# Three edits to a fused attention and two-MLP kernel: scale of w1 from a sum of squares, the product with the values in float16 halves, and a new table of ranks

## The chip, the cores and the metric

The kernel runs on one core of a Trainium2 chip. The metric is the device time of one execution in microseconds (us); lower is better. Before the change the median of three runs is 1182.09 us (1180.85 to 1185.35).

## The reference

Inputs q, k, v have the shape (8 batches, 8 heads, 576 rows, 64). All is float32.

```python
# chunked attention: 9 chunks of 64 rows, each attends to itself only
scores = (q_c @ k_c.T) / 8
attn = exp(scores - max); attn = attn / (sum(attn) + 1e-9)
x = attn @ v_c                              # to (8, 576, 512), heads side by side
# first MLP
xn = (x - mean) / sqrt(var + 1e-6) * g1
x = x + relu(xn @ w1) @ w2                  # w1: 512 x 2048, w2: 2048 x 512
# second MLP with a gate along the rows
h = gelu_tanh(x @ w_in); u, v = halves of h
v = norm(v) * g2;  v = w_sg @ v + b_sg      # w_sg: 576 x 576
out = x + (u * v) @ w_out
```

## The kernel before, in words

The 4608 rows of x are 36 tiles of 128 rows (`t`), two to a block of 256 rows (`b`, 18 blocks). A float32 matrix that enters a large product is split into two float16 halves, high and low, and a product is three float16 products: high by high, high by low, low by high. From block 4 on the first MLP, and in the second MLP the product with w_in, run as seven products of half the size (the lists `POS` and `SIDES`). One function builds the program. Nothing is issued in the order of the source: `op(engine, ns, fn, rd, wr, prio)` (L59) records each step with its engine, an assumed duration, what it reads and writes, and a rank. `Plan.run` (L88) then plays the steps through by the assumed durations and, at each time when an engine is free, issues the ready step with the lowest rank. The ranks of the first eight tiles and of the weight pieces stand in the table `TUNE` (L24 to 42). Every engine runs its own list in order, so a step that waits holds all later steps of its engine.

**Attention** (`attention`, L300 to 437). For a tile, q and k arrive by a DMA, 16 products of 64 by 64 give the scores in PSUM (`qk`, L291), VectorE takes row maxima and subtracts them (L371, L372), ScalarE takes the exponential (L375). The result must be turned for the product with v. Up to tile 13, TensorE does it (`pt_`, L334) and ScalarE copies it from PSUM (L396). From tile 14 on (22 tiles) ScalarE rounds it to float16 (the high half of `ph`), VectorE makes the low half (L383), a DMA transposes both (`ptt`, L386), and VectorE adds the halves to a float32 tile again (`pt`, L389). The product with v (`pv_`, L343) is 16 float32 products of 64 by 64, each of which TensorE runs as two passes, each with a weight load of its own. They use the four 64 by 64 quadrants of the array: partitions 0 to 63 or 64 to 127 of the operands by partitions 0 to 63 or 64 to 127 of the output. The row sums are taken by VectorE (L393), or for tiles 0 to 3 by a product with a column of ones (`sums`, L366); a reciprocal (L360) and a product (L410) give x. `norm` (L439) computes mean and variance (L442, L443), the inverse root on POOL (GpSimd, L437, L440), the normalized tile on VectorE or POOL (L446), its two float16 halves (L449, L451), and a DMA transposes them to `xT` (L266). From tile 10 on the product with v of one tile and the scores of the next are one step.

**w1** (`make_w1`, L481). Eight pieces of 256 columns. A piece arrives as raw 64-bit words and is converted by ScalarE and VectorE (L466, L471). For its scale, ScalarE (L489, seven pieces) or VectorE sums or bounds the magnitudes on each partition. `par` (L243) makes one number of the 128: a product with the unit matrix that turns the column to a row (`turn`, L223), a maximum on VectorE (`rowmax`, L227), a product that spreads it to 128 partitions (`spread`, L231), a copy (`floor`, L239). VectorE cuts it to a power of two, takes its reciprocal and scales g1 with it (L257, L258, L501). Then the piece is multiplied by that column and split into `w1h` and `w1l` (L510, L514 in the direct form). `scale_w2` (L556) later uses the pieces' scales for w2.

**The first product** (`ff1`, L596) takes 12 products of 128 by 128 by 256 for each group of 128 columns; two groups use one piece. Where the planner sees TensorE idle in the start, `busy` (L1162) puts products of zeros (L1165), one for each 150 ns of the expected idle time beyond 400 ns, until the third PSUM bank is used the first time (`plan.idle = None`). From there on none is added.

Of the kernel before, what the change touches and what calls it, by code (L numbers as in the profile page):

```python
# [9 lines left out]
F16 = mybir.dt.float16  # L10
# [14 lines left out]
    a=[2264, -1991, -1698, -26, -1734, 4025, 2562, -374],  # L25
    w=[2426, 2508, 9, 2951, 1823, 2431, -436, 2455],
    w2=[2013, 747, 2422, -1063, 2355, -444, 700, 2423],
    an=[-135, -91, -57, -1323, -88, -1232, 366, 0],
    wb=[0, -1141, 0, -402, 109, -61, 1242, 1022],
    lo=[1, 0, 0, 0, 0, 1, 1, 1],  # L30
    wl=[1, 1, 1, 1, 1, 1, 1, 0],
    wc=[0, 1, 0, 1, 1, 1, 0, 1],
    wa=[1, 1, 1, 1, 0, 1, 1, 1],
    wm=[0, 0, 1, 0, 0, 0, 0, 1],
    ps=[1, 1, 1, 1],
    wf=[1, 1, 1, 1, 1, 0, 0, 1],
# [110 lines left out]
def fused_kernel(ctx: ExitStack, tc, qkv, w1, w2, g1, w_in, w_out, wsgt, wsgs, g2, b_sg, out):  # L147
    nc = tc.nc
    PSUM = bass.MemoryType.PSUM
    P = 128  # L150
# [46 lines left out]
    g1m = small.tile([P, 2], F32, name="g1m")  # L197
    redw = small.tile([P, 8], F32, name="redw")
    invw = small.tile([P, 8], F32, name="invw")
    gsw = small.tile([P, 8, 4], F32, name="gsw")  # L200
    e1c = small.tile([P, 8], F32, name="e1c")
# [99 lines left out]
    def attention(t):  # L301
# [22 lines left out]
        pt = palloc("pt", 1, [P, 4, 128], F32)  # L324
# [5 lines left out]
        pv = s2[:, :, 256:512].rearrange("p a (h d) -> p a h d", h=4)  # L330

# [6 lines left out]
        def pv_():  # L338
            for hp in range(4):
# [38 lines left out]
        else:  # L378
            ph = palloc("ph", 1, [P, 2, 512], F16)
            ptt = palloc("ptt", 1, [P, 2, 512], F16)  # L380
# [38 lines left out]
    def norm(t, x, o):  # L419
# [16 lines left out]
        def rs_():  # L436
# [7 lines left out]
        o("POOL", 730, rs_, rd=[mv, "cpow"], wr=[rs], two=2)  # L444
        xe = ("POOL", 830, nc.gpsimd) if t < 8 and TUNE['xn'][t] else ("DVE", 460, nc.vector)
        o(xe[0], xe[1], lambda: xe[2].tensor_scalar(  # L446
            out=xn.t, in0=x.t, scalar1=mv.t[:, 0:1], scalar2=rs.t, op0=ALU.subtract, op1=ALU.mult
        ), rd=[x, mv, rs], wr=[xn], two=1 + (xe[0] == "POOL"))
# [32 lines left out]
    def make_w1(j):  # L481
# [4 lines left out]
        e, inv, gs = e1c[:, j:j + 1], invw[:, j:j + 1], gsw[:, j]  # L486
        wv = lambda: w.t.rearrange("p (k f) -> p k f", k=4)
        if TUNE['wa'][j]:
            op("ACT", 1056, lambda: nc.scalar.activation(  # L489
                out=w1h[j].bitcast(BF16), in_=wv(), func=AF.Abs, scale=g1m[:, 1:2], accum_out=redw[:, j:j + 1]  # L490
            ), rd=[w, "g1m"], wr=[f"mxw{j}", f"w1h{j}"], prio=pr)
        else:
            op("DVE", 1127, lambda: absmax(redw[:, j:j + 1], w.t), rd=[w], wr=[f"mxw{j}"], prio=pr)
            op("DVE", 78, lambda: nc.vector.tensor_tensor(
                out=redw[:, j:j + 1], in0=redw[:, j:j + 1], in1=g1m[:, 0:1], op=ALU.mult
            ), rd=["g1m"], wr=[f"mxw{j}"], prio=pr)
# [1154 lines left out]
```

## Time and profile before

| | us |
|---|---|
| median of three runs | 1182.09 |
| lowest and highest run | 1180.85, 1185.35 |
| the profiled execution: its own time | 1181.42 |
| its span in the profile | 1179.6 |
| TensorE products (PE), busy in the span | 1168.0 |
| VectorE (DVE) | 866.1 |
| ScalarE (ACT) | 564.2 |
| GpSimd (POOL) | 268.3 |

Busy time is the time in which an instruction of the engine runs. Products on PE are pipelined: their starts are recorded, their ends are modelled, so a row's duration is longer than its distance to the next start. The distance of starts is what a product costs where PE never stops. PE stands for products, PEld for weight loads, which run beside them.

### The profile page before, as it was taken

How to read it: one execution, taken by the hardware profiler on the slowest of the kernel's cores; microseconds unless marked ns; L12 is line 12 of the kernel's file. 1: busy time of each engine (PE TensorE's matmuls, PEld its weight loads, DVE VectorE, ACT ScalarE, POOL GpSimd, SP SyncE). 2: the span in 40 equal slices, each digit the busy share in tenths (PEclk: the TensorE clock that was granted, in tenths of full speed). 3: DMA queues.
4: the chain of work that ended last, by engine and by line, in shares of the span. 5: the costliest groups of instructions: out<-in, count | busy, mean ns of one | idle time of the engine just before them, and what ended most of it. 6: DMA issues, size and time to landing. Idle time of an engine off the chain costs nothing.

```text
span 1179.6 us, 26988 instructions
## 1 busy us (share of the span) xinstructions
PE 1168.0 (99%) x11387; PEld 879.9 (75%) x11387; DVE 866.1 (73%) x1673; ACT 564.2 (48%) x830; POOL 268.3 (23%) x318
## 2 busy tenths in 40 slices
PE   8899999999999999999999999999999999999998
PEld 6688654688888888888888888888565556556454
DVE  6996114999898898888877775677899479477455
ACT  5787501555655665644344334445646335434330
POOL 2213401434312322331221312013303102202300
PEclk6999999999999999999999999999999999999999
DMA  7974002135572433343234221435284473262203
GB/s 278 282 239 126 1 18 81 64 108 156 164 161 67 82 86 76 88 95 93 84 81 91 55 55 28 87 89 167 57 176 128 102 147 112 87 124 73 89 1 116
DMA packets 165049, 124.30 MB, mean 105 GB/s; under 512 B 128704, under 2 KB 137792, under 8 KB 164928
## 3 DMA queue, kind: packets, MB, share of 16 engines
q1 hardware_dynamic: 164928, 122.58, 39.6%
q8 instruction: 89, 1.46, 0.5%
q14 instruction: 32, 0.26, 0.1%
HBM read 72.74 MB, written 18.88 MB: 78 GB/s over the span
## 4 chain that ended last, share of the span: by engine, by line
PE 96%; DVE 2%; DMA 1%; issue 0%; ACT 0%; SPq 0%; POOL 0%; DVEq 0%; ACTq 0%
PE bank L722 25%; PE acc L774 22%; PE bank L615 6%; PE pb L1446 5%; PE acc L1530 4%; PE pair L636 4%; PE bank L636 4%; PE pb L1530 4%; PE acc L1446 3%; PE pb L1350 3%; PE acc L1392 3%; PE pb L1392 3%; PE acc L1350 3%; PE pair L343 2%; PE pair L291 2%; PE pb L1447 1%
## 5 line engine op out<-in xcount | busy, mean ns | idle before, releaser
L722 PE MATMUL bank<-xT,w1h 128*128 128x256 f16 x1792 | 299.7, 273 | 0.0
L774 PEld LDWEIGHTS <-arena 128*128 128x128 f16 x2352 | 228.3, 98 | 27.6
L722 PE MATMUL bank<-xT,w1l 128*128 128x256 f16 x896 | 244.2, 273 | 0.0
L774 PE MATMUL acc<-w,arena 128*128 128x256 f16 x1344 | 202.7, 273 | 0.0
L722 PEld LDWEIGHTS <-w1h 128*128 128x128 f16 x1792 | 175.0, 98 | 20.5
L749 ACT ACTIVATE arena<-arena 128x896 f16<-128x896 f32 x112 | 106.3, 949 | 144.2 <-PE acc L774 84.8
L774 PE MATMUL acc<-w2s,arena 128*128 128x256 f16 x1008 | 165.4, 273 | 0.0
L750 DVE TENSOR_TENSOR arena<-arena 128x896 f16<-128x896 f32 x112 | 122.3, 1092 | 30.2 <-ACT arena L749 29.7
L737 ACT ACTIVATE arena<-bank 128x512 f32<-128x512 f32 x112 | 66.6, 594 | 129.7 <-PE bank L722 122.8
L722 PEld LDWEIGHTS <-w1l 128*128 128x128 f16 x896 | 87.7, 98 | 10.2
L615 PE MATMUL bank<-xT,w1h 128*128 128x256 f16 x512 | 86.2, 273 | 1.3 <-DMA xT<-hl 1.1
L807 POOL TENSOR_TENSOR x<-x,u 128x256 f32<-128x256 f32 (+1 forms) x60 | 53.5, 921 | 124.9 <-DVE x L797 89.4
L744 DVE TENSOR_TENSOR arena<-arena 128x256 f32<-128x256 f32 x112 | 54.7, 489 | 32.2 <-ACT arena L737 31.9
L437 POOL TENSOR_SCALAR rs<-mv 128x1 f32<-128x1 f32 x36 | 11.3, 313 | 284.0 <-DVE mv L443 267.3
L1350 PEld LDWEIGHTS <-x2T 128*128 128x128 f16 x672 | 65.6, 98 | 9.1 <-issue 0.2
L451 POOL TENSOR_TENSOR hl<-xn,hl 128x512 f16<-128x512 f32 x32 | 49.8, 1555 | 89.0 <-ACT hl L449 85.7
L615 PE MATMUL bank<-xT,w1l 128*128 128x256 f16 x256 | 69.8, 273 | 0.0
L615 PEld LDWEIGHTS <-w1h 128*128 128x128 f16 x512 | 48.6, 98 | 12.2 <-issue 1.6
L1446 PEld LDWEIGHTS <-vh 128*128 128x128 f16 x288 | 28.5, 99 | 33.4
L1530 PEld LDWEIGHTS <-gh 128*128 128x128 f16 x296 | 28.9, 98 | 31.6
L1297 POOL TENSOR_SCALAR rs<-mv 128x2 f32<-128x2 f32 (+1 forms) x20 | 5.8, 291 | 204.3 <-DVE mv L1292 204.1
L1446 PE MATMUL pb<-wsg,vh 128*128 128x512 f16 x166 | 51.6, 380 | 0.0
(300 smaller groups left out, 2293.0 us busy)
## 6 DMA issues: line engine op xcount, KB each, us to landing
straw<-in_w SPq DMA_DIRECT2D x16, 1023.8 KB, 5.7
qkl<-in_qkv SPq DMA_DIRECT2D x26, 512.0 KB, 4.0
x2d<-x SPq DMA_DIRECT2D x36, 256.0 KB, 2.1
xr<-x2d SPq DMA_DIRECT2D x35, 256.0 KB, 2.9
out<-xr SPq DMA_DIRECT2D x35, 256.0 KB, 3.1
xs<-x2d SPq DMA_DIRECT2D x27, 256.0 KB, 3.6
vl<-in_qkv SPq DMA_DIRECT2D x26, 256.0 KB, 3.2
qk<-in_qkv SPq DMA_DIRECT2D x10, 512.0 KB, 5.5
```

Source lines behind the costliest of these rows:

```text
L615: nc.tensor.matmul(acc, lhsT=w[j][:, k, fc], rhs=xT.t[:, x, k], start=(n == 0), stop=(n == 11))
L636: nc.tensor.matmul(acc[i], lhsT=h[x].t[:, c], rhs=w2t[j][:, f % 2, y], start=(f == 0 and n == 0), stop=(f == NF - 1 and n == 2),)
L722: nc.tensor.matmul(acc[:, y * 256:y * 256 + 256], lhsT=w[j][:, k, fc], rhs=xT.t[:, x, k], start=(n == 0), stop=(n == 11),)
L737: op("ACT", 500, lambda: nc.scalar.activation(out=o.t[:, 0:4].rearrange("p n t -> p (n t)"), in_=acc, func=AF.Relu, scale=0.5), rd=[kb] + ...
L744: nc.vector.tensor_tensor(out=two(6, 8), in0=two(1, 3), in1=two(0, 2), op=ALU.subtract)
L749: op("ACT", 860, lambda: nc.scalar.activation(out=h.t[:, 0], in_=o.t[:, 1:8], func=AF.Copy), rd=[o] + ar, wr=[h], prio=-100)
L750: op("DVE", 1010, lambda: nc.vector.tensor_tensor(out=h.t[:, 1], in0=o.t[:, 1:8], in1=h.t[:, 0], op=ALU.subtract), rd=[o, h], wr=[h.key + ...
L774: nc.tensor.matmul(acc, lhsT=h.t[:, x, n], rhs=r(y), start=(first and j == 0 and m == 0), stop=(j == 7 and m == 2), skip_group_check=True,)
L1350: nc.tensor.matmul(ap[:, q * 256:q * 256 + 256], lhsT=xT[:, x, a, k, c], rhs=right(b, 1, k, w), start=(first and n == 0), stop=(k == 1 and ...
L1392: nc.tensor.matmul(ap, lhsT=right(b, 0, k, w)[:, m * 128:m * 128 + 128], rhs=xT[:, x, a, k], start=(first and n == 0), stop=(k == 1 and w ...
L1446: nc.tensor.matmul(ap, lhsT=v[:, fc], rhs=w[:, 0:512], start=(n == 0), stop=end)
L1530: nc.tensor.matmul(ap[:, 0:m], lhsT=x[:, k, c], rhs=w[:, k, fc], start=(n == 0), stop=(n == 11))
```

## The change

Four edits, and new numbers in `TUNE`:

1. The scale of a w1 piece is taken from the sum of squares. ScalarE squares all eight pieces; one product with a 128 by 128 matrix of ones (`total`) adds the 128 partitions and leaves the sum on all of them; VectorE bounds it from below, POOL raises it to the power -0.5, VectorE scales g1. `turn`, `rowmax`, `spread` and the cut to a power of two go for w1; they stay for w2's one scale.
2. Of four of the first eight tiles the reciprocal of the row sums moves to POOL (`rp`, where the row sums come from VectorE), and for three the normalized tile is made on ScalarE (`xa`).
3. From tile 14 on the two transposed float16 halves are not added. v is split into float16 halves (`vq`: one copy on ScalarE, one subtraction on VectorE), and the product with v is three float16 products for each float32 one: 48 weight loads and 48 products in a tile where 16 float32 products of two passes stood.
4. Two of the first four tiles take their row sums by TensorE instead of four (`ps`).

```diff
 TUNE = dict(
-    a=[2264, -1991, -1698, -26, -1734, 4025, 2562, -374],
-    w=[2426, 2508, 9, 2951, 1823, 2431, -436, 2455],
+    a=[2627, 508, -2387, -855, 341, 2595, 604, 4055],
+    w=[3820, 3377, 142, 4188, 5125, 3910, 106, 2633],
...
-    ps=[1, 1, 1, 1],
-    wf=[1, 1, 1, 1, 1, 0, 0, 1],
+    xa=[0, 1, 0, 0, 0, 1, 0, 1],
+    rp=[0, 1, 1, 1, 0, 1, 1, 1],
+    ps=[0, 1, 0, 1],
+    wf=[1, 1, 1, 1, 0, 0, 0, 1],
...
         def pv_():
+            if t >= BYDMA:
+                for hp in range(4):
+                    for n, (y, z) in enumerate(((0, 0), (0, 1), (1, 0))):
+                        for r in (slice(0, 64), slice(64, 128)):
+                            for c in range(2):
+                                k = c * 256 + hp * 64
+                                q = hp * 128 + c * 64
+                                nc.tensor.matmul(
+                                    s2[64 * c:64 * c + 64, r.start // 64, 256 + hp * 64:256 + hp * 64 + 64],
+                                    lhsT=ptt[0].t[r, y, q:q + 64],
+                                    rhs=vq[0].t[r, z, k:k + 64],
+                                    start=(n == 0),
+                                    stop=(n == 2),
+                                )
+                return
...
-            ), rd=[ph], wr=[ptt], lat=3500)
+            ), rd=[ph], wr=[ptt[0]], lat=3500)
+            vq[0] = palloc("vq", 1, [P, 2, 512], F16)
+            o("ACT", 520, lambda: nc.scalar.activation(out=vq[0].t[:, 0], in_=v.t, func=AF.Copy), rd=[v], wr=[vq[0]])
             o("DVE", 600, lambda: nc.vector.tensor_tensor(
-                out=pt.t.rearrange("p h q -> p (h q)"), in0=ptt.t[:, 0], in1=ptt.t[:, 1], op=ALU.add
-            ), rd=[ptt], wr=[pt], two=1, **far)
+                out=vq[0].t[:, 1], in0=v.t, in1=vq[0].t[:, 0], op=ALU.subtract
+            ), rd=[v], wr=[vq[0]], two=1, **far)
...
+                def rp_():
+                    f = lambda x: x.t.rearrange("p h a o -> p (h a o)")
+                    nc.gpsimd.tensor_scalar(out=f(sm), in0=f(sm), scalar1=1.0, scalar2=1e-9, op0=ALU.mult, op1=ALU.add)
+                    nc.gpsimd.tensor_tensor(out=f(rd), in0=f(sm), in1=cneg.to_broadcast([P, 8]), op=ALU.pow)
...
-        if TUNE['wa'][j]:
-            op("ACT", 1056, lambda: nc.scalar.activation(
-                out=w1h[j].bitcast(BF16), in_=wv(), func=AF.Abs, scale=g1m[:, 1:2], accum_out=redw[:, j:j + 1]
-            ), rd=[w, "g1m"], wr=[f"mxw{j}", f"w1h{j}"], prio=pr)
...
-        par(e, redw[:, j:j + 1], [f"mxw{j}"], [f"e{j}"], pr)
-
-        def scale():
-            top2(e, inv)
-            nc.vector.tensor_scalar(out=gs, in0=g1s, scalar1=inv, scalar2=32.0, op0=ALU.mult, op1=ALU.mult)
-
-        op("DVE", 520, scale, wr=[f"e{j}"], prio=pr, two=1)
+        op("ACT", 1056, lambda: nc.scalar.activation(
+            out=w1h[j].bitcast(BF16), in_=wv(), func=AF.Square, scale=g1m, accum_out=redw[:, j:j + 1]
+        ), rd=[w, "g1m"], wr=[f"mxw{j}", f"w1h{j}"], prio=pr)
...
+        op("PE", 200, lambda: total(scr, redw[:, j:j + 1]), rd=[f"mxw{j}", "ident"], wr=[k], prio=top, lat=300)
+        op("DVE", 80, lambda: nc.vector.tensor_scalar_max(q, scr[:, P:P + 1], 2.0 ** -120), rd=[k], wr=[f"q{j}"], prio=top)
+        op("POOL", 560, lambda: nc.gpsimd.tensor_tensor(
+            out=inv, in0=q, in1=cpow, op=ALU.pow
+        ), rd=[f"q{j}", "cpow"], wr=[f"i{j}"], prio=top, two=2)
+        op("DVE", 240, lambda: nc.vector.tensor_scalar(
+            out=gs, in0=g1s, scalar1=inv, scalar2=1024.0, op0=ALU.mult, op1=ALU.mult
+        ), rd=[f"i{j}"], wr=[f"e{j}"], prio=pr, two=1)
```

What it moves on TensorE shows at three places. **The scale of a piece**, between two groups of `ff1` (`bank` is a group's accumulator, `redw` the 128 partial sums, `rowm` the maximum). Before:

```order
L615 LDWEIGHTS w1l_159
L615 MATMUL bank_69<-xT,w1l_159 128x256
L223 MATMUL bank_70<-ident,redw 1x128
L231 MATMUL bank_70<-rowm,ones 128x1
L615 LDWEIGHTS w1h_152
```

and with the change:

```order
L657 LDWEIGHTS w1l_161
L657 MATMUL bank_69<-xT,w1l_161 128x256
L239 MATMUL bank_70<-redw,ones 128x1
L657 LDWEIGHTS w1h_154
L657 MATMUL bank_68<-xT,w1h_154 128x256
```

Two float32 products of a piece, the second of which waits for VectorE's maximum, are one, which waits for ScalarE's sum alone.

**The start of the first product** on TensorE, from the step ahead of its first group. Before, the row of the maximum stands ahead of it, and further on three groups and five products with v (L343) are through when piece 1 (`w1h_150`) is first used:

```order
L1165 MATMUL bank_71<-zero 128x256
L231 MATMUL bank_70<-rowm,ones 128x1
L343 MATMUL pair_66<-v,pt 64x64 x16
L615 LDWEIGHTS w1h_149
...
L223 MATMUL bank_70<-ident,redw 1x128
L615 LDWEIGHTS w1h_150
```

and with the change:

```order
L657 MATMUL bank_68<-xT,w1l_159 128x256
L364 MATMUL pair_67<-v,pt 64x64 x16
L657 LDWEIGHTS w1h_153
...
L294 MATMUL pair_67<-qk 64x64 x16
L239 MATMUL bank_70<-redw,ones 128x1
L657 LDWEIGHTS w1h_152
```

Piece 2 (`w1h_153`) comes ahead of piece 1 (`w1h_152`). Ahead of the fourth group stand seven score products and six products with v, where six and five stood.

**The product with v** of a tile from 14 on, in the steady state. Before:

```order
L774 LDWEIGHTS arena
L774 MATMUL acc_2782<-w_2_167,arena 128x256
L343 MATMUL pair_67<-vl,pt 64x64 x16
L291 MATMUL pair_67<-qkl 64x64 x16
L774 LDWEIGHTS arena
```

and with the change, where the pair of rows of L352 stands 48 times:

```order
L816 MATMUL acc_2732<-w2s_2511,arena 128x256
L352 LDWEIGHTS ptt
L352 MATMUL pair_67<-vq,ptt 64x64
...
L294 MATMUL pair_67<-qkl 64x64 x16
L816 LDWEIGHTS arena
```

The products' place between the groups and ahead of the next tile's scores is the same; their kind and number differ.

## Rows read from the trace of the kernel before

**Rows 1.** The page's part 1: busy time, share and instructions of each engine.

```profile
PE 1168.0 (99%) x11387; PEld 879.9 (75%) x11387; DVE 866.1 (73%) x1673; ACT 564.2 (48%) x830; POOL 268.3 (23%) x318
```

**Rows 2.** Busy time by stretch; columns: length, each engine's busy us, PEclk, DMA.

```profile
30.00:40.00 10.00, 7.86 (x117) 5.92 (x115) 9.46 (x24) 6.90 (x12) 4.35 (x8) 1.00 1.14 272
50.00:60.00 10.00, 10.00 (x141) 7.92 (x138) 9.75 (x25) 8.11 (x16) 0.00 (x0) 1.00 0.74 264
400.00:500.00 100.00, 100.00 (x1183) 88.97 (x1182) 87.64 (x170) 57.48 (x79) 29.69 (x30) 1.00 0.36 85
```

**Rows 3.** PE's timeline in the start: start, duration, line, instruction, [idle before, releaser].

```profile
27.23 0.76 PE L366 MATMUL bank<-onec,pt 64*64 64x1 f32 x32
27.84 0.66 PE L343 MATMUL pair<-v,pt 64*64 64x64 f32 x32
28.43 0.38 PE L223 MATMUL bank<-ident,redw 128*1 128x128 f32 x2
...
33.73 0.38 PE L231 MATMUL bank<-rowm,ones 1*128 1x1 f32 x2 [1.21 <-DVE rowm L227]
...
34.67 0.39 PE L615 MATMUL bank<-xT,w1h 128*128 128x256 f16 x2
...
42.13 0.38 PE L223 MATMUL bank<-ident,redw 128*1 128x128 f32 x2 [0.99 <-ACT w1h L489]
...
45.05 0.39 PE L615 MATMUL bank<-xT,w1h 128*128 128x256 f16 x2 [1.13 <-DMA xT<-hl]
```

**Rows 4.** PE's timeline, two small products between groups of the first product.

```profile
59.76 0.38 PE L223 MATMUL bank<-ident,redw 128*1 128x128 f32 x2
60.07 0.38 PE L231 MATMUL bank<-rowm,ones 1*128 1x1 f32 x2
60.38 0.39 PE L615 MATMUL bank<-xT,w1h 128*128 128x256 f16 x2
```

**Rows 5.** PE's timeline, a product with ones (L236) among float16 products.

```profile
881.84 0.28 PE L236 MATMUL acc<-red,ones 128*128 128x1 f32 x2
881.98 1.47 PE L1350 MATMUL pb<-winT,x2T 128*128 128x256 f16 x12
```

**Rows 6.** PE's timeline in the steady state, around one product with v.

```profile
431.23 0.69 PE L343 MATMUL pair<-vl,pt 64*64 64x64 f32 x32
431.74 0.65 PE L291 MATMUL pair<-qkl 64*64 64x64 f32 x32
432.32 0.50 PE L774 MATMUL acc<-w,arena 128*128 128x256 f16 x3
```

**Rows 7.** Weight loads by shape: busy us and mean ns of one, idle before.

```profile
L774 PEld LDWEIGHTS <-arena 128*128 128x128 f16 x2352 | 228.3, 98 | 27.6
L343 PEld LDWEIGHTS pair<-vl,pt 64*64 64x64 f32 x832 | 14.5, 134 | 5.7 <-issue 3.0 <-DVE arena L744 1.3 <-DVE winT L892 0.4
L334 PEld LDWEIGHTS pair<-ident,pml 128*128 128x128 f32 x16 | 1.9, 141 | 0.2
L223 PEld LDWEIGHTS bank<-ident,redw 128*1 128x1 f32 x16 | 0.8, 81 | 2.8 <-ACT w1h L489 1.9 <-issue 0.4 <-ACT hl L449 0.2
```

**Rows 8.** PE's timeline, a float16 product of 64 columns (L1447) and the next.

```profile
843.94 0.19 PE L1447 MATMUL pb<-wsg,vh 128*128 128x64 f16 x1
843.97 0.38 PE L1446 MATMUL acc<-wsg,vh 128*128 128x512 f16 x1
```

**Rows 9.** DVE's addition of the transposed halves (L389): ns min/median/max, first and last start.

```profile
L389 DVE TENSOR_TENSOR pt<-ptt x22: 678/683/1649, 292.8 to 690.8; 128x512 f32<-128x512 f16 x22
```

More of the change, by code (lines that the diff above doesn't have):

```diff
@@ L196, in fused_kernel @@
     x2mx = small.tile([P, NT], F32, name="x2mx")
-    g1m = small.tile([P, 2], F32, name="g1m")
+    g1m = small.tile([P, 1], F32, name="g1m")
+    cneg = small.tile([P, 1], F32, name="cneg")
     redw = small.tile([P, 8], F32, name="redw")
@@ L200, in fused_kernel @@
     gsw = small.tile([P, 8, 4], F32, name="gsw")
+    q1c = small.tile([P, 8], F32, name="q1c")
     e1c = small.tile([P, 8], F32, name="e1c")
@@ L330, in attention @@
         pv = s2[:, :, 256:512].rearrange("p a (h d) -> p a h d", h=4)
+        ptt, vq = [None], [None]
+        pp = lambda: [pt, v] if t < BYDMA else [ptt[0], vq[0]]
         def pt_():
@@ L444, in norm @@
         o("POOL", 730, rs_, rd=[mv, "cpow"], wr=[rs], two=2)
-        xe = ("POOL", 830, nc.gpsimd) if t < 8 and TUNE['xn'][t] else ("DVE", 460, nc.vector)
-        o(xe[0], xe[1], lambda: xe[2].tensor_scalar(
-            out=xn.t, in0=x.t, scalar1=mv.t[:, 0:1], scalar2=rs.t, op0=ALU.subtract, op1=ALU.mult
-        ), rd=[x, mv, rs], wr=[xn], two=1 + (xe[0] == "POOL"))
+        if t < 8 and TUNE['xa'][t]:
+            nb = palloc("nb", 2, [P, 1], F32)
+            o("POOL", 200, lambda: nc.gpsimd.tensor_scalar(
+                out=nb.t, in0=mv.t[:, 0:1], scalar1=rs.t, scalar2=-1.0, op0=ALU.mult, op1=ALU.mult
+            ), rd=[mv, rs], wr=[nb], two=2)
+        xe = ("POOL", 830, nc.gpsimd) if t < 8 and TUNE['xn'][t] else ("DVE", 460, nc.vector)
+        if t < 8 and TUNE['xa'][t]:
+            o("ACT", 520, lambda: nc.scalar.activation(
+                out=xn.t, in_=x.t, func=AF.Identity, scale=rs.t, bias=nb.t
+            ), rd=[x, nb, rs], wr=[xn])
+        else:
+            o(xe[0], xe[1], lambda: xe[2].tensor_scalar(
+                out=xn.t, in0=x.t, scalar1=mv.t[:, 0:1], scalar2=rs.t, op0=ALU.subtract, op1=ALU.mult
+            ), rd=[x, mv, rs], wr=[xn], two=1 + (xe[0] == "POOL"))
         o("ACT", 520, lambda: nc.scalar.activation(out=hl.t[:, 0], in_=xn.t, func=AF.Copy), rd=[xn], wr=[hl])
@@ L559, in a @@
         def a():
+            nc.vector.tensor_tensor(out=e1c, in0=q1c, in1=invw, op=ALU.mult)
             u = m2c.bitcast(U32)
@@ L570, in b @@
             )
-            nc.vector.tensor_scalar_mul(col("c2"), e, 2.0 ** -19)
-            for k, y in enumerate((2.0 ** -18, 2.0 ** -16, -(2.0 ** -16))):
+            nc.vector.tensor_scalar_mul(col("c2"), e, 2.0 ** -24)
+            for k, y in enumerate((2.0 ** -23, 2.0 ** -21, -(2.0 ** -21))):
                 nc.vector.tensor_scalar_mul(col(f"c2{'abn'[k]}"), e, y)
-        op("DVE", 485, a, rd=[f"m2c{j}" for j in range(8)] + [f"e{j}" for j in range(8)], wr=["red"], prio=pr)
+        op("DVE", 620, a, rd=[f"m2c{j}" for j in range(8)] + [f"e{j}" for j in range(8)], wr=["red"], prio=pr)
         par(col("w2_e"), red, ["red"], ["w2_r"], pr)
```

57 lines of the change are left out of this document (28 added, 29 removed).

## The prediction
> **What bounds the kernel now.** I read the busy times first, then the stretches, then TensorE's timeline where it stops. TensorE is busy for 99% of the span, the next engine, DVE, for 73% [rows 1]. The stretches say where the missing per cent lies: from 30 to 40 us PE is busy for 7.86 of 10 us, from 50 us on for all of it, and so still from 400 to 500 us [rows 2]. So the kernel has two parts. Up to 45 us PE waits for the first tiles and the first weight pieces, and DVE at 9.46 of 10 us is the engine that keeps it waiting. After the wait that ends at 45.05 us [rows 3] PE never stops for long, and what is worth anything there is PE's own time: work taken from DVE, ACT or POOL gives nothing, and a product taken from PE gives its distance of starts.
>
> The time therefore changes by three terms: what PE's start gains or loses, what the small products for w1's scale cost, and what the product with v costs in 22 tiles. The sum is made against the profiled execution, 1181.42 us, which lies 0.67 us below the median of the runs. A change of 0.5% (5.9 us) is about what a measurement of this kernel can tell from none.
>
> **The start.** PE's last three waits there are 1.21 us for DVE's row maximum of a piece, 0.99 us for ACT's sum and 1.13 us for a transposing DMA, 3.33 us in all [rows 3]. The first goes with the change: the one product of a piece now needs ACT's sum only. The new order also puts one more score product and one more product with v ahead of the fourth group, that is, into a stretch in which PE waits anyway, and so takes them from the stretch in which it doesn't. A product with v cost 0.59 us here (27.84 to 28.43) [rows 3], the scores 0.58 (431.74 to 432.32) [rows 6]: about 1.1 us together. That makes 1.21 + 1.1 = 2.3 us less.
>
> It is not more because DVE hardly gets relief. Up to the low half of the third piece, DVE's list holds 28 passes over a 512-wide tile where it held 25, four normalizations where it held three, and 21 small steps where it held 37: two row sums come back from TensorE, and that outweighs most of the small steps that go. The two row sums taken from PE are worth nothing, as PE waits there. The POOL steps (eight powers, four reciprocals) land on an engine that is 23% busy, the extra ScalarE passes on one that is 48% busy [rows 1]; each has slack, but the chain of a piece now crosses POOL between two DVE steps, and DVE's later steps queue behind a late one. The number of products of zeros, which shows the idle time that the planner expected, is 64 where it was 63, so by its own count there is no gain at all; it stops counting at the third bank, which now comes earlier. Bounds: if the other two waits go as well, -2.3 - 2.12 = -4.4 us; if all three come back at other places on top of the present ones, +3.3. I take -2.3.
>
> **The small products.** Of the products that turn and spread a piece's sum, four turns and five spreads stand behind the start in the old order. Each takes 0.31 us of PE (59.76, 60.07, 60.38) [rows 4]: 9 × 0.31 = 2.8 us. In the new order four products with ones stand there. The same shape took 0.14 us among float16 products (881.84 to 881.98) [rows 5]: 0.56 us. The term is -2.2 us, and nothing hides it, because PE is the bound. If the product with ones cost 0.31 too, it would be -1.6; that is its upper end, and -2.8 the lower.
>
> **The product with v.** It took 0.51 us in float32 (431.23 to 431.74) [rows 6]: 16 products of two passes, spread over four quadrants, so eight rounds of four. What sets a round is the weight load. The product with a column of ones has one moving column instead of 64 and took 0.61 us against 0.59 for the one with v right behind it (27.23, 27.84, 28.43) [rows 3], so the moving columns are free. A float32 load of 64 columns lasts 134 ns, one of a single column 81 [rows 7]; the difference, 53 ns, times eight rounds is 0.43 us, and 0.08 us is left for the beginning and the end. In float16 there are 48 products, 12 rounds. What such a load of 64 columns costs in a quadrant no row shows. A float16 load of 128 columns into the whole array lasts 98 ns, only 17 more than the single column, and even the float32 load for a transpose takes 141, or 60 more for 128 columns [rows 7], which is 30 for 64. A float16 product of 64 columns takes 0.03 us of PE (843.94 to 843.97) [rows 8]. If a round costs these 0.03, the tile costs 12 × 0.03 + 0.08 = 0.44 us, 0.07 less than now, and 22 tiles -1.5 us. Without the 0.08 it would be 0.36 and -3.3 us: the lower end. If a round costs 53 ns as in float32, 12 × 0.053 + 0.08 = 0.72 us, 0.21 more, and 22 tiles +4.6 us. If the quadrants did not overlap at all, 48 × 0.03 = 1.44 us, 0.93 more, +20.5 us: the far end. I take -1.5, because both loads that are no float32 products lie near 0.03.
>
> DVE's addition (22 × 0.68 us [rows 9]) goes, and a subtraction of the same width comes, made as soon as v is there. The addition was the last step ahead of the product; PE runs at 100.00 of 100 us in this stretch [rows 2], so its going frees nothing. The 22 copies of v on ACT run beside work on an engine at 57 of 100 us [rows 2]; if that cover went, the copy would still be early, since v needs no softmax.
>
> **Sum.** -2.3 - 2.2 - 1.5 = -6.0 us: 1175.4 for the profiled execution, 1176.1 against the median.
>
> **The rivals.** *The loads bind.* The float16 loads of 64 columns go at the float32 pace, 53 ns in a round. For it: the present rounds are set by loads, and the number of loads rises from 32 to 48. Against it: the two other kinds of load. Then -2.3 - 2.2 + 4.6 = +0.1 us: 1182.2, no change. The Trainium skill speaks for this one: "TensorE: Matmul & The Clock Gate", section on LDWEIGHTS, gives a load columns/1.2 ns, an estimate of 53 ns for 64 columns, and "TensorEngine Tiling (Array Packing)", Restrictions and Gotchas, says that column tiling excludes the fast weight load. By it the product with v would cost +4.6 us as above; for float32 the trace agrees (53 ns), for float16 in quadrants no run here shows it.
>
> *The quadrants don't overlap in float16*, or PE can't be fed with 96 instructions in half a microsecond; the place is the 22 products with v. For it: each float32 product made its two passes from one instruction, and now every load and every product is an instruction. Against it: the loads and products around it run ahead of need, and PE's list can be filled while the group before runs. Price: +20.5 us, in sum -2.3 - 2.2 + 20.5 = +16.0: 1198.1, slower. It decides from 0.5 us more for a tile: (5.9 + 4.5)/22 = 0.47.
>
> *The start gives nothing.* The ranks were set by assumed durations; DVE's work up to the third piece stays as large, and a late power on POOL puts a new wait where the row maximum was. Then 0 - 2.2 - 1.5 = -3.7 us: 1178.4; with the upper end of the start, +3.3, it is -0.4: 1181.7, no change. Against it: PE no longer waits for a DVE step that queues behind others.
>
> **How the numbers follow.** Chances: forecast 0.55, loads bind 0.20, start gives nothing 0.12, no overlap 0.09, anything else 0.04. The forecast's own range is 1171 to 1181: its terms at their lower ends make -4.4 - 2.8 - 3.3 = -10.5 us (1171.6), with the start at zero and the rest as taken it is 1178.4. The bound for faster, 1176.2, cuts through it: 0.37 of its 0.55 is faster, 0.18 the same. The start rival gives 0.03 faster, 0.08 the same, 0.01 slower; the loads 0.01 faster, 0.18 the same, 0.01 slower; no overlap is 0.09 slower; the rest 0.01, 0.01 and 0.02. That makes faster 0.42, same 0.45, slower 0.13. The range for 8 in 10 runs from 1170 to 1187: it takes in the loads with a start that gives nothing (0 - 2.2 + 4.6 = +2.4, 1184.5) and leaves out the far end.
>
> **What would show it.** In the profile of the changed kernel: the product with v at about 431 us should take 0.44 us from its first start to the first start of the scores; 0.7 says that the loads bind, over 1.0 that the quadrants don't overlap. A product with ones between groups should take 0.14 us. PE should end its last wait of over 0.9 us before 45 us, with three groups of the first product, seven score products and six products with v done by then, and never wait for a row maximum of a piece of w1. From 50 to 700 us PE should stay at 100%. The prediction is wrong if PE waits there again, for instance for a low half of a piece or for the halves of v, or if a tile's product with v is outside 0.36 to 0.72 us.

## The result and the profile after

The changed kernel takes 1189.8 us (median of six runs, 1188.11 to 1191.6) beside 1182.93 for the one before (six runs, 1180.85 to 1185.35). The ratio is 1.0059, with a 95% interval of 1.0042 to 1.0075: slower by about 7 us, and above the predicted range. The profiled execution took 1191.4 us, with a span of 1189.6 (before 1181.42 and 1179.6).

The page's part 1 of the changed kernel, which answers [rows 1]:

```profile
PE 1163.2 (98%) x11660; PEld 875.8 (74%) x11660; DVE 868.3 (73%) x1635; ACT 578.7 (49%) x850; POOL 280.4 (24%) x344
```

PE is busy 4.8 us less, as intended, and stands idle for 1189.6 - 1163.2 = 26.4 us where it stood for 1179.6 - 1168.0 = 11.6. So 14.8 us of new idle time eat 4.8 us of saved work. Where it lies, the stretches show (columns as in [rows 2]: length, PE, PEld, DVE, ACT, POOL, PEclk, DMA):

```profile
30.00:40.00 10.00, 8.13 (x79) 6.22 (x78) 8.49 (x21) 5.59 (x11) 3.18 (x4) 0.73 0.85 237
40.00:50.00 10.00, 7.50 (x105) 5.54 (x103) 7.93 (x18) 5.81 (x11) 4.60 (x5) 0.83 1.04 263
50.00:60.00 10.00, 9.69 (x141) 8.44 (x139) 9.01 (x21) 8.74 (x18) 5.10 (x8) 1.00 1.05 311
60.00:70.00 10.00, 6.83 (x62) 5.81 (x59) 4.93 (x12) 7.49 (x13) 7.54 (x12) 1.00 0.97 235
70.00:80.00 10.00, 7.26 (x90) 5.83 (x87) 7.43 (x14) 5.76 (x12) 7.70 (x6) 1.00 0.69 235
400.00:500.00 100.00, 100.00 (x1266) 88.89 (x1265) 87.47 (x176) 58.17 (x81) 23.66 (x27) 1.00 0.38 82
```

Before, PE had no wait over 0.15 us from 50 us on. Now it loses 5.9 of 20 us from 60 to 80, where POOL is the engine with most work. PE's timeline names the waits (start, duration, line, instruction, idle before and releaser); the first rows answer [rows 3]:

```profile
32.58 0.59 PE L657 MATMUL bank<-xT,w1h 128*128 128x256 f16 x2 [1.03 <-DMA xT<-hl]
...
44.82 0.69 PE L294 MATMUL pair<-qk 64*64 64x64 f32 x32 [2.50 <-DVE x L442]
...
61.96 0.66 PE L340 MATMUL pair<-ident,pm 128*128 128x128 f32 x4 [1.24 <-ACT pm L396]
...
68.78 0.38 PE L657 MATMUL bank<-xT,w1h 128*128 128x256 f16 x2 [1.65 <-DVE latela L662]
...
78.04 0.38 PE L657 MATMUL bank<-xT,w1h 128*128 128x256 f16 x2 [2.60 <-DVE latelb L662]
...
354.01 0.58 PE L352 MATMUL pair<-vq,ptt 64*64 64x64 f16 x48 [0.74 <-DMA ptt<-ph]
...
562.33 0.58 PE L352 MATMUL pair<-vq,ptt 64*64 64x64 f16 x48 [1.86 <-DMA ptt<-ph]
```

The first group of the first product does come earlier (32.58 instead of 34.67 us) and the wait for the row maximum is gone. A wait of 2.50 us ends at 44.82 us, about where the old order's last one ended. But the waits did not end there: 1.24, 1.65 and 2.60 us follow, and two more in the steady state.

Who made the two longest, the chain of waits in order of time tells (start, duration, what):

```profile
40.12 1.21 POOL rs L469
...
42.32 1.73 POOL rd L422
...
44.08 0.70 DVE x L442
...
44.82 0.69 PE pair L294 x32
45.52 0.31 PE bank L239 x2
45.83 4.37 PE bank L657 x24
...
58.67 7.94 DMA straw<-in_w
...
71.11 5.07 POOL cw L572 x4
...
76.20 1.06 ACT w1h L577
77.26 0.28 ACT latehb L661
...
77.56 0.42 DVE latelb L662
```

The last link of the first is the reciprocal of eight row sums as a power on POOL: 1.73 us for that one instruction, where the planner assumes 0.76 for it and an addition. DVE's product for x waits for it, and PE's scores wait for x. POOL came to it late, too: ahead of it in POOL's list stands the first step of an inverse root (L469), which took 1.21 us beside a pass of DVE over two tensors that starts at 40.05, and 0.19 at 32.14. The second is POOL's multiplication of a piece of w1, four instructions: 5.07 us, assumed 1.86. ScalarE's rounding of the piece waits for it, the drains of PE's banks queue behind that, and PE waits for a bank. The same four instructions took 1.84 us at 65.86, while DVE was idle; in the 5.07 us DVE ran three passes over two 1024-wide tensors. Its timeline (start, duration, line, instruction):

```profile
40.05 1.22 DVE L513 SCALAR_TENSOR_TENSOR cw<-straw,top 128x1024 uint32<-128x1024 uint32 x1
...
71.19 1.21 DVE L513 SCALAR_TENSOR_TENSOR cw<-straw,top 128x1024 uint32<-128x1024 uint32 x1
72.32 0.41 DVE L662 SCALAR_TENSOR_TENSOR latelb<-bank,latehb 128x256 f16<-128x256 f32 x1
72.65 1.21 DVE L513 SCALAR_TENSOR_TENSOR w<-straw,top 128x1024 uint32<-128x1024 uint32 x1
73.78 1.21 DVE L579 TENSOR_TENSOR w1l<-cw,w1h 128x1024 f16<-128x1024 f32 x1
```

The difference, 5.07 - 1.84 = 3.2 us, is nearly their 3.6 us. The Trainium skill says why ("SBUF — State Buffer", section "SBUF: two separate sides"): VectorE with two inputs in SBUF and GpSimd share one pair of ports as an exclusive lock, and the loser blocks; these rows agree.

The wait of 1.65 us ahead of 68.78 has another maker. ScalarE stood still for a raw piece, whose DMA took 7.94 us to land (58.67 to 66.61 in the chain above; the planner reckons 5.2), and the drain of PE's bank stood behind it in ScalarE's list (ScalarE's timeline):

```profile
66.69 1.35 ACT L508 ACTIVATE top<-straw 128x1024 f16<-128x1024 bf16 x1 [2.43 <-DMA straw<-in_w]
67.91 0.36 ACT L661 ACTIVATE lateha<-bank 128x256 f16<-128x256 f32 x1
```

The clock adds to the waits. After the 2.50 us stop PE ran 24 products in 4.37 us, with a granted clock of 0.83 from 40 to 50 us: the first 15 of them stood at twice their normal distance, 1.2 instead of 2.4 GHz, some 1.6 us more. That is a matter of the single execution: behind the same stop of 2.50 us the granted clock was 1.00 in e3, f3 and h4 below.

To place the loss I use two marks on PE that every kernel has: the first product of the first second-stage accumulator (`acc`), which ends the start, and the first product with `winT`, which ends the steady state. Before, then after:

```profile
231.00 0.49 PE L774 MATMUL acc<-w,arena 128*128 128x256 f16 x3
...
805.75 4.09 PE L1350 MATMUL pb<-winT,x2T 128*128 128x256 f16 x36
```

```profile
238.04 0.49 PE L816 MATMUL acc<-w,arena 128*128 128x256 f16 x3
...
813.93 1.26 PE L1389 MATMUL pb<-winT,x2T 128*128 128x256 f16 x10
```

So the start costs 7.0 us more, the steady state 575.89 - 574.75 = 1.1, and the rest 375.7 - 373.9 = 1.8, of which 1.3 is one wait for DVE in the second MLP; of the other traces only e2's has such a one.

The 7.0 us of the start all lie behind 45.2 us. By then both kernels have done three groups of the first product, and the changed one is a product with v ahead. Behind it (columns as above; before, then after):

```profile
45.20:80.00 34.80, 34.75 (x355) 28.90 (x354) 31.94 (x77) 30.05 (x60) 5.55 (x8) 1.00 0.75 254
80.00:231.00 151.00, 151.00 (x1263) 96.77 (x1260) 72.76 (x149) 60.46 (x101) 37.75 (x30) 1.00 0.24 71
```

```profile
45.20:80.00 34.80, 28.57 (x335) 23.59 (x324) 26.03 (x54) 24.18 (x44) 21.26 (x27) 0.95 0.91 257
80.00:238.04 158.04, 156.73 (x1234) 101.90 (x1232) 72.32 (x146) 67.62 (x113) 39.68 (x30) 1.00 0.22 68
```

PE stands idle for 7.5 us where it stood for less than 0.1. It is busy for 0.45 us less, and since 1.6 us of that time are the lower clock, some 2 us of its work there have gone.

### The profile page after: what moved, and what is told of

It is laid out like the page before. It is cut to its first block, busy times and chain, and to the rows that moved or that the text cites. A ratio compares the mean times of both kernels' runs of the same rounds, so it can differ in the third digit from the quotient of the medians.

```text
span 1189.6 us, 27584 instructions
## 1 busy us (share of the span) xinstructions
PE 1163.2 (98%) x11660; PEld 875.8 (74%) x11660; DVE 868.3 (73%) x1635; ACT 578.7 (49%) x850; POOL 280.4 (24%) x344
## 4 chain that ended last, share of the span: by engine, by line
PE 85%; DVE 6%; DMA 3%; issue 3%; ACT 1%; POOL 1%; SPq 0%; ACTq 0%; DVEq 0%; POOLq 0%
PE bank L764 22%; PE acc L816 19%; PE pb L1485 5%; PE acc L1569 4%; PE bank L657 4%; PE pair L678 4%; PE bank L678 3%; PE pb L1569 3%; PE acc L1485 3%; PE pb L1431 3%; PE acc L1431 3%; PE pb L1389 3%; PE acc L1389 2%; DMA straw<-in_w 2%; PE pair L294 1%
## 5 line engine op out<-in xcount | busy, mean ns | idle before, releaser
L786 DVE TENSOR_TENSOR arena<-arena 128x256 f32<-128x256 f32 x112 | 53.3, 476 | 25.1 <-ACT arena L779 24.4
L493 POOL TENSOR_TENSOR hl<-xn,hl 128x512 f16<-128x512 f32 x33 | 46.6, 1411 | 83.6 <-ACT hl L491 83.6
L469 POOL TENSOR_SCALAR rs<-mv 128x1 f32<-128x1 f32 x36 | 14.1, 390 | 189.2 <-DVE mv L475 188.7
L787 DVE TENSOR_TENSOR arena<-arena 128x256 f32<-128x256 f32 x112 | 55.3, 493 | 3.8
```

Source lines behind the costliest of these rows:

```text
L787: nc.vector.tensor_tensor(out=two(4, 7), in0=two(0, 6), in1=two(2, 8), op=ALU.add)
```

## The experiments

The table gathers them: median of all runs, ratio to the kernel before on the same chip with its 95% interval, and from one profiled execution each the start, the steady state and, within it, PE's waits over 0.15 us.

| kernel | us | ratio | start | steady | waits in it |
|---|---|---|---|---|---|
| before | 1182.9 | | 231.0 | 574.8 | 0 |
| changed | 1189.8 | 1.0059 (1.0042, 1.0075) | 238.0 | 575.9 | 2.6 |
| e1 | 1183.5 | 1.0001 (0.9992, 1.0010) | 233.0 | 574.4 | 0.9 |
| e2 | 1182.8 | 0.9996 (0.9986, 1.0006) | 231.9 | 573.8 | 0.6 |
| e3 | 1188.4 | 1.0039 (1.0025, 1.0053) | 236.7 | 574.6 | 0 |
| e4 | 1189.8 | 1.0053 (1.0038, 1.0068) | 239.6 | 576.1 | 2.6 |
| f1 | 1186.8 | 1.0026 (1.0011, 1.0041) | 238.0 | 573.8 | 0.6 |
| f2 | 1189.5 | 1.0038 (1.0020, 1.0055) | 237.8 | 575.1 | 1.6 |
| f3 | 1189.6 | 1.0049 (1.0034, 1.0065) | 235.5 | 576.8 | 3.2 |
| f4 | 1184.2 | 1.0006 (0.9995, 1.0017) | 231.9 | 574.2 | 0.5 |
| g1 | 1184.2 | 1.0013 (1.0001, 1.0025) | 233.5 | 576.8 | 3.4 |
| g2 | 1187.9 | 1.0045 (1.0030, 1.0060) | 233.2 | 578.8 | 4.0 |
| g3 | 1188.6 | 1.0057 (1.0039, 1.0076) | 235.7 | 576.9 | 3.6 |
| g4 | 1197.4 | 1.0129 (1.0114, 1.0144) | 243.1 | 578.3 | 4.5 |
| h1 | 1186.0 | 1.0027 (1.0015, 1.0040) | 232.6 | 578.3 | 3.2 |
| h2 | 1186.1 | 1.0032 (1.0018, 1.0047) | 230.2 | 578.9 | 3.6 |
| h3 | 1196.1 | 1.0116 (1.0099, 1.0132) | 236.8 | 582.6 | 7.1 |
| h4 | 1190.4 | 1.0069 (1.0053, 1.0086) | 236.9 | 577.0 | 3.7 |
| i1 | 1188.9 | 1.0055 (1.0036, 1.0075) | 240.6 | 577.3 | 3.8 |
| i2 | 1191.8 | 1.0065 (1.0043, 1.0088) | 234.8 | 581.3 | 5.8 |

A profile is one execution, and those of one kernel differ by 3 us and more; for i1 it is a long one (1194.0), for f4 its shortest (1181.8).

### Which edit costs: e1, e2, e3

**e1**, the changed code with the old table:

```diff
-    a=[2627, 508, -2387, -855, 341, 2595, 604, 4055],
+    a=[2264, -1991, -1698, -26, -1734, 4025, 2562, -374],
...
-    xa=[0, 1, 0, 0, 0, 1, 0, 1],
-    rp=[0, 1, 1, 1, 0, 1, 1, 1],
+    xa=[0]*8,
+    rp=[0]*8,
```

> All code edits of the change, but with the table of ranks from before (no reciprocal on POOL, no normalized tile on ScalarE, row sums of four tiles by TensorE). Theory A (the new ranks and the POOL placements lose in the start, the edits themselves gain): the start gets back its 7.1 us, the waits of 2.50 and 2.60 us before 80 us are gone; the rest stays: 1189.8 - 7.1 = about 1182.7 us, and if the small products give their 2 us, 1181. Theory B (the new chain of the scale over POOL delays the weight pieces whatever the ranks): 1188 us or more, with PE waits of over 1 us for a piece's scale between 40 and 80 us. Theory C (the float16 product with v costs the time): 1187 or more, with the loss after 230 us.

1183.52 us, the same as before. Theories B and C fall: neither the new chain of the scale nor the float16 product needs 7 us. Theory A holds in its first half, the loss came with the table; in its second it doesn't, as the edits gained nothing. PE waits for ScalarE's sum and for a bank in the start (PE's timeline of e1):

```profile
44.64 0.38 PE L240 MATMUL bank<-redw,ones 128*128 128x1 f32 x2 [1.91 <-ACT w1h L531]
...
55.05 0.38 PE L658 MATMUL bank<-xT,w1h 128*128 128x256 f16 x2 [2.19 <-DVE latelb L663]
```

**e2**, the kernel before with the edit of the product with v alone:

```diff
-            o("PE", 1260 * z, pv_, rd=[pt, v], wr=[kp])
+            o("PE", 1260 * z, pv_, rd=pp(), wr=[kp])
```

(`pp` and the float16 branch of `pv_` as in the change.)

> The kernel before with the float16 product with v alone. Theory A: the start as before (last group of blocks 0 to 3 ends at 156.6 us); 22 products with v at 0.41 instead of 0.51 us give -2.2, the scores behind them at 0.63 instead of 0.58 cost +1.1, and waits for the transposing DMA such as the 0.74 and 1.86 us of the changed kernel cost about +2.6: 1182.9 - 2.2 + 1.1 + 2.6 = 1184.4 us, no measurable change. Theory C: 1188 us or more. Theory B says the same as A here.

1182.8 us, the same. Its start is that of before within 1 us, its steady state 1.0 us shorter in spite of 0.55 us of waits, and one wait of 1.36 us in the second MLP, as in the changed kernel, offsets that.

**e3**, the changed kernel with the old product with v:

```diff
-            if t >= BYDMA:
+            if t >= 99:
...
-        pp = lambda: [pt, v] if t < BYDMA else [ptt[0], vq[0]]
+        pp = lambda: [pt, v]
```

> The changed kernel with the product with v in float32 again and the addition of the two transposed halves on DVE. Theory A: the start stays as in the changed kernel, PE's waits for the transposing DMA at 354 and 562 us go, the products get 0.1 us longer each: 1189.8 - 1.5 = about 1188.3 us, and still slower than before by 5 us. Theory C: all of the loss goes, 1183 us.

1188.36 us, as theory A said. In the steady state no wait is left; the start keeps its 2.50 us wait and ends at 236.66 us. As in e1, the loss sits in the start and comes with the table. That it ends 1.4 us earlier than the changed kernel's is the clock: PE's idle time behind 45.2 us is the same 7.5 us, but the granted clock was 1.00 in the 5 us behind the stop, where it was 0.66 in the changed kernel.

### Which part of the table: e4, f1, f2, f3

**e4** (`rp=[0]*8` in the changed kernel):

> The changed kernel with the reciprocals of the row sums on VectorE again for all tiles (rp all 0). Theory A in its particular form (the eight-value power on POOL, 1.7 us where 0.76 was assumed with its addition, makes the wait of 2.50 us at 44.8 us and takes the clock down behind it): the wait shrinks below 1 us and two groups run at full clock: -2 to -4 us, 1186 to 1188 us. Rival (the new table as a whole is at fault, no single step): another wait takes its place, 1189 to 1191 us.

1189.82 us. The wait for x did not shrink, it grew (e4's timeline of PE):

```profile
42.77 1.13 PE L294 MATMUL pair<-qk 64*64 64x64 f32 x32 [3.81 <-DVE x L442]
```

This doesn't clear the power, since the planner made another order. x was there 2.06 us sooner (it starts at 42.02 instead of 44.08), but PE had stood since 38.96, and the first group of the first product began at 44.27 instead of 32.58. What the run shows is that taking the power from POOL doesn't pay under these ranks; what the power alone costs stays open.

**f1** keeps the new numbers and takes the old choices of engine and form, **f2** the reverse:

```diff
-    rp=[0, 1, 1, 1, 0, 1, 1, 1],
+    rp=[0, 0, 0, 0, 0, 0, 0, 0],
...
-    ps=[0, 1, 0, 1],
+    ps=[1, 1, 1, 1],
...
-    xn=[0, 1, 0, 0, 0, 1, 1, 1],
+    xn=[0, 1, 0, 0, 1, 1, 1, 1],
```

> The changed kernel with its rank numbers (a, w, w2, an, wb, wd, w2d, f), but with the eight lists that choose an engine or a form (lo, wl, wc, wm, ps, wf, xn and the new rp and xa) as before. Theory A1 (the choice of engines is at fault: POOL has 45.8 us of work in the first 100 us instead of 25.2, and its steps run longer than assumed beside VectorE): the start gets back most of its 7 us, 1183 to 1185 us. Theory A2 (the order by the new numbers is at fault): 1188 us or more.

> The reverse: the rank numbers of before, the choices of engine and form of the changed kernel. Theory A1: 1188 us or more. Theory A2: 1183 to 1185 us. If both this and the other half are slow, numbers and choices only fit together, and any mismatch of a table with its choices costs several us.

1186.84 and 1189.52 us, and both starts end near 238 us. Neither half alone is at fault: the new numbers lose with the old choices, and the old numbers with the new ones, the outcome that the second expectation names last. But the new numbers and the new choices lose together as well, so only the old pair is seen to fit.

**f3**, no piece multiplied on POOL:

```diff
-    wf=[1, 1, 1, 1, 0, 0, 0, 1],
+    wf=[1, 1, 1, 1, 1, 1, 1, 1],
```

> The changed kernel with pieces 4 to 6 of w1 in the direct form (ScalarE scales and rounds from the unscaled piece, VectorE makes the low half), so that POOL multiplies no piece and makes no low half. Theory A1 in its particular form (the multiplications on POOL, 1.84 to 5.06 us where 1.86 was assumed, make the waits of 1.65 us at 68.8 and 2.60 us at 78.0 us): both waits below 1 us, -3 us, 1186 to 1187 us. Rival: ScalarE or VectorE becomes late in their place, 1189 to 1191 us.

1189.62 us. The waits at 68.8 and 78.0 us do go, and the start ends some 1.2 to 2.6 us earlier than in e3 and the changed kernel (235.45). But the order shifts as well, and the profile shows 3.2 us of waits in the steady state, 2.11 of them at one product with v. For the wait at 78.0 the chain above names the step; the one at 68.8 came from the raw piece, and e3 has no such wait either, with that multiplication at 2.92 us. Taking the step away did not pay.

### What the planner assumes: f4, g1, g2, g3, h4, h3

**f4** (g1 the first line alone, g2 the second; g3 with 400 and 1000; h4 with 700 and 1800):

```diff
-                o("POOL", 760, rp_, rd=[sm, "cpow"], wr=[sm, rd], two=2)
+                o("POOL", 1950, rp_, rd=[sm, "cpow"], wr=[sm, rd], two=2)
...
-        op(("ACT", "POOL")[TUNE['wc'][j]], (1600, 1860)[TUNE['wc'][j]], mul, rd=[f"e{j}"], wr=[w], prio=back, two=2 * TUNE['wc'][j])
+        op(("ACT", "POOL")[TUNE['wc'][j]], (1600, 3240)[TUNE['wc'][j]], mul, rd=[f"e{j}"], wr=[w], prio=back, two=2 * TUNE['wc'][j])
```

> The changed kernel where the planner assumes what the trace measured: 1.95 us for the two steps of the reciprocal on POOL (0.76 before) and 3.24 us for the multiplication of a piece on POOL (1.86 before; the mean of 2.81, 1.84 and 5.06). Ranks and choices are kept, the order that comes out differs. If the short assumptions are the cause, the planner now fills the time with other work: 1186 to 1188 us. If the numbers were fitted to the old assumptions and only the whole fits, 1189 to 1192 us.

1184.15 us: the loss is gone, more than expected, with every edit of the change in place.

> The changed kernel where the planner assumes 1.95 us for the reciprocal on POOL (0.76 before); the multiplication of a piece stays at 1.86. Theory A3 (the planner's too short durations on POOL are the cause): part of the 6 us comes back, the wait of 2.50 us for x at 44.8 us above all: 1186 to 1188 us. Rival L (any other order would be as good, the changed kernel's is one unlucky draw): 1184 to 1186, and the same for every other pair of assumptions.

> The changed kernel where the planner assumes 3.24 us for the multiplication of a piece on POOL (1.86 before); the reciprocal stays at 0.76. Theory A3: the waits of 1.65 and 2.60 us near 70 and 78 us go, 1186 to 1188 us. Rival L: 1184 to 1186 us.

> The control: assumptions still further from the trace, 0.40 us for the reciprocal and 1.00 for the multiplication. Theory A3: no better than the changed kernel, 1189 to 1193 us. Rival L: the order differs as much as with the measured durations, so 1184 to 1187 us.

> The second control: 0.70 us for the reciprocal and 1.80 for the multiplication, near the changed kernel's 0.76 and 1.86. The order on TensorE differs in 590 of 19902 rows. Theory A3: 1188 to 1191 us, as the changed kernel. Rival L: the order still differs somewhere in the start, so it may fall anywhere from 1184 to 1190 us.

1184.24, 1187.94, 1188.62 and 1190.42 us. Up to here theory A3 looked right: the more of the two durations was true, the earlier the start ended (235.7 and 236.9 for the controls, 233.5 and 233.2 with one, 231.9 with both). The times follow less well: g1 alone is as good as f4, and g2 hardly better than the control g3. The next run refuted it in its general form. **h3**, all of POOL's steps near what the trace shows in the mean (FAST is shown; the durations of f4, 0.64 for the power of a piece and 0.27 for the bias go with it):

```diff
-    ("POOL", 730): 789, ("POOL", 1110): 1157, ("POOL", 830): 2070,
+    ("POOL", 730): 1170, ("POOL", 1110): 1250, ("POOL", 830): 2950,
...
```

> The changed kernel where every step on POOL has the duration that its trace shows: besides 1.95 and 3.24 us also 1.17 us for the two steps of the inverse root (0.79 before), 2.95 for a normalized tile (2.07), 1.25 for a low half of a tile (1.16), 0.64 for the power of a piece (0.56), 0.27 for the bias (0.20). Theory A3: a third order, again without the loss, 1182 to 1185 us, the start's end (first product of the second stage's loop) at 230 to 233 us. Rival L: anywhere from 1184 to 1190 us, no better than the run with two durations corrected.

1196.08 us, slower than the changed kernel. The waits changed place again (h3's timeline of PE):

```profile
46.59 0.59 PE L657 MATMUL bank<-xT,w1h 128*128 128x256 f16 x2 [3.07 <-DMA xT<-hl]
...
293.06 0.28 PE L816 MATMUL acc<-w,arena 128*128 128x256 f16 x1 [2.31 <-DVE arena L792]
...
404.14 0.58 PE L352 MATMUL pair<-vq,ptt 64*64 64x64 f16 x48 [3.11 <-DMA ptt<-ph]
```

Truer durations on one engine do not make a better order by themselves. One number can't be true for these steps anyway: the step L469 took 0.19 us and 1.21, the four multiplications 1.84 and 5.07, by what DVE ran beside them.

### Longer assumptions for transfers: g4, h1, h2, i1, i2

The float16 product waits for its transposing DMA itself. Of 22 such transfers the changed kernel shows (trace of the tile `ptt`):

```profile
DMA to landing us min/median/max: 3.0/3.1/8.5
```

The planner reckons 1.1 + 3.5 = 4.6 us from SP's start. **h1** is f4 with 5.5 for the 3.5, **h2** is e2 with it, **g4** is h1 with `wl` of piece 6 at 1:

```diff
-            ), rd=[ph], wr=[ptt[0]], lat=3500)
+            ), rd=[ph], wr=[ptt[0]], lat=5500)
```

> A version that may beat both: the measured POOL durations (1.95 and 3.24), 5.5 us instead of 3.5 assumed from the transposing DMA of a tile from 14 on to its product with v, and the low half of piece 6 on VectorE instead of POOL. The run with the measured durations alone took 1184.15 us and had waits of 1.62 us for that low half, 0.50 for the transposing DMA and 2.50 for xT. Theory A3: the first two go, 1181 to 1183 us. Rival L: 1184 to 1187.

> The measured POOL durations and 5.5 us assumed from the transposing DMA to the product with v, without the low half of piece 6 on VectorE: tells which of the two added edits made the combined version take 1197.37 us. If the low half on VectorE did it (it pushed the scale of w2 back, with waits of 2.90, 1.79 and 1.83 us between 117 and 132 us): 1183 to 1184 us here, and no wait for that DMA. If the longer latency did it (its steps crowd into the same stretch): 1192 us or more.

> The kernel before with the float16 product with v alone and 5.5 us assumed from the transposing DMA. If the waits for that DMA (0.55 us in the run without it) are all that the new product costs: 0.5 us below that run, ratio to before 0.9985 to 0.9995. If the later place of the product makes other steps late: 1184 us or more.

1197.37, 1186.04 and 1186.06 us: none gains. The wait for that DMA goes in g4 and shrinks in h1 (0.21 us, 0.50 in f4); in h2 it does not (0.71, 0.55 in e2). Others come (h2's timeline of PE):

```profile
397.41 0.59 PE L742 MATMUL bank<-xT,w1h 128*128 128x256 f16 x2 [2.16 <-issue]
```

What held PE there the profile doesn't show. The greater part of g4's loss came with the low half on VectorE, as h1 without it shows: waits of 2.90, 1.79 and 1.83 us near 120 us, the second for DVE's part of w2's scale.

**i1** is f4, **i2** is e2, both with

```diff
-        o("SP", 1100, lambda: transpose(xT.t, slice(c0, c0 + 128), hl.t), rd=[hl], wr=[xT], lat=2200)
+        o("SP", 1100, lambda: transpose(xT.t, slice(c0, c0 + 128), hl.t), rd=[hl], wr=[xT], lat=4200 if t < 8 else 2200)
```

> The run with two POOL durations as measured (1184.15 us), and 4.2 us instead of 2.2 assumed from the issue of the first eight transposing DMAs to xT to their landing. If that assumption makes the wait of 2.50 us for xT at 44.7 us: the wait goes below 1 us, the start ends near 230 us instead of 231.9, 1182 to 1183 us. If orders fall by luck: 1184 to 1192 us, with another wait of 2 us or more in the start.

> The kernel before with the float16 product with v alone (1182.8 us, ratio 0.9996) and the same longer assumption for xT. If the assumption is what matters: its wait of 0.95 us for xT at 45.1 us goes, 1181.5 to 1182.5 us. If orders fall by luck: 1183 to 1190 us.

1188.91 and 1191.75 us. The waits for xT near 45 us go in both, and yet the time rises, by their ratios some 6 us from f4 to i1 and 8 from e2 to i2. i2 is the clearest case, since its code is that of e2 and its assumption the truer one: from SP's start it reckons 5.3 us, and the seven transfers to xT that the changed kernel issues in the first 100 us landed after 5.3 in the median (4.9 to 9.4). It waits 4.13 us at a single product (i2's timeline of PE):

```profile
356.54 0.58 PE L349 MATMUL pair<-vq,ptt 64*64 64x64 f16 x48 [4.13 <-DMA ptt<-ph]
```

No version beat the kernel before; e1, e2 and f4 equal it.

## Why the prediction was wrong

**The start** is the step that failed: -2.3 with an upper end of +3.3, while the start ended 7.0 us later. Up to 45 us it went about as forecast: three groups were done, the sixth product with v and, at 44.82 us, the seventh scores. I derived both ends from the three waits that the old order had, and took it that PE would stop waiting at 45 us as before. The waits that decide come behind it, at places where the old order had none: 7.5 us of idle time up to the first `acc`, and 1.6 us for the clock, against some 2 us of saved work. The sentence that each of POOL's new steps "has slack", with POOL 23% busy, was the wrong use of an average: a power of eight values takes 1.7 us and four multiplications up to 5.07 us there, in an in-order list with a chain behind it. The prediction's list of these steps was short, too: besides the powers and reciprocals, `wf`, `wc` and `wl` put the multiplications of three pieces on POOL instead of one, and a low half. The profile of before had a sign: DVE ran 9.46 and 9.75 of 10 us in the stretches read there [rows 2], and an engine so full cannot make up a step that waits 1.54 us for POOL, as x did ahead of 44.08 us. But DVE is not what keeps PE waiting throughout, as the prediction had it: of the three waits in [rows 3] one is DVE's, and behind the new ones stand POOL, ScalarE and a DMA as well. The rival "the start gives nothing" named a late power on POOL, a link of the first chain, and priced it too low (1181.7 at most).

**The small products.** The mechanism is right, the size about: the product with ones took these distances (PE's timeline of the changed kernel):

```profile
64.20 0.28 PE L239 MATMUL bank<-redw,ones 128*128 128x1 f32 x2
64.34 0.38 PE L657 MATMUL bank<-xT,w1h 128*128 128x256 f16 x2
...
73.73 0.38 PE L239 MATMUL bank<-redw,ones 128*128 128x1 f32 x2
73.97 0.38 PE L657 MATMUL bank<-xT,w1h 128*128 128x256 f16 x2
```

0.14 us as forecast, and 0.24. "Nothing hides it, because PE is the bound" failed: between 45 and 80 us PE waited, and e1, where the new chain of the scale alone changes the start, ends it 2 us later than before, not 2.2 earlier.

**The product with v** was right in its time. Its rows answer [rows 6], its loads [rows 7]:

```profile
435.65 0.58 PE L352 MATMUL pair<-vq,ptt 64*64 64x64 f16 x48
436.06 0.70 PE L294 MATMUL pair<-qkl 64*64 64x64 f32 x32
436.68 0.50 PE L816 MATMUL acc<-w2s,arena 128*128 128x256 f16 x3
```

```profile
L352 PEld LDWEIGHTS <-ptt 64*64 64x64 f16 x1056 | 10.2, 108 | 7.4 <-issue 4.2 <-DMA ptt<-ph 3.2
```

0.41 us where I forecast 0.44 and it was 0.51; the scores behind it take 0.62 instead of 0.58. That is (-0.10 + 0.04) × 22 = -1.3 us. With its waits taken off, the steady state is 573.2 to 573.7 us in 13 of the 18 traces with this product, against 574.8: -1.1 to -1.5, as predicted. In the other five (g2, h1, h2, h3, i2) it is 574.8 to 575.5, and in each of them the granted clock stood at 0.66 to 0.70 in the 5 us in which PE went on after a stop of 2.2 to 4.1 us. Stops of 2.1 to 3.5 us in f3, g4, h4 and i1 left it at 1.00. The rival "the loads bind" wanted 0.72 us and falls, "the quadrants don't overlap" with 1.44 falls too. With the first falls, as the price of a round in float16, the rule of the Trainium skill quoted there ("TensorE: Matmul & The Clock Gate", section on LDWEIGHTS), an estimated 53 ns for 64 columns: by that rule 12 rounds would take an estimated 0.64 us, and the whole took 0.41. The working behind the forecast is not shown by its coming out. A load lasts 108 ns, 27 more than that of a single column, but 48 such loads in 0.41 us are 12 or 13 at a time, so neither these 27 ns nor the 53 ns of float32 is read off as the price of a round. What failed is the sentence on DVE's addition, that "its going frees nothing": it freed PE to run into the transposing DMA. Addition and assumed latencies had put the product late enough: in the kernel before it starts 7.2 us or more after the issue of its transfer, and no transfer landed after more than 5.1 us. In the changed one it starts 4.2 us or more after it, and the two waits stand at landings of 6.1 and 5.7. PE waited for that DMA in every trace with the float16 product but g4's, 0.2 to 4.8 us in all.

**Their sum.** Start +7.0, with the small products in it, steady state -1.5 + 2.6, the rest +1.8: 10.0 us between the two profiles, about 7 between the medians.

**What stays open.** That the new table makes the loss is shown (e1). Which wrong assumption, if any single one, makes its order wait is not: two corrected durations cured it, and one of them did as well; all of POOL's corrected did worse, and longer latencies of transfers, for xT a truer one, harmed a good order. So f4's recovery may be the correction or a fortunate order.

## What to carry to other kernels

Where a planner's table fixes the order, a change of numbers is a change of its own and has to be priced with its own range: changes of assumption alone moved this kernel between 1184 and 1196 us, while the edits of the code under the old table changed the time by nothing measurable (e1, e2). Time code edits with the old table first (e1, e2), and a new table by itself. When an engine's step disappears, ask what it was padding: an addition of 0.7 us, with what the planner allowed around it, had kept 3 us between a product and a DMA whose landing spreads.

## What the hardware showed that was not expected

- A power on POOL took 0.55 us for one value on a partition and 1.65 to 1.73 for eight. The step with a multiplication and an addition took 0.19 us for one value and 0.20 for eight.
- POOL's multiplication of a piece took 1.84 us beside an idle VectorE and 5.07 beside three of its two-tensor passes. A step on one value a partition went from 0.19 to 1.21 us beside one such pass.
- 48 float16 products of 64 by 64 by 64 in four quadrants run in 0.41 us with all their loads, 8.5 ns for each.
- A transposing DMA of the same tile landed after 3.1 us in the median, and once after 8.5.
